# Block-sum attention with a top-1 mixture of experts on one core: route work ahead of the minimum, drains behind gathers, one test that ends the pairs, outputs scaled ahead of the last weight splits

## The chip, the cores and the metric

One Trainium2 chip, one core of it. The metric is the device time of one execution in microseconds; times before and after are medians over several executions. The engines are named as the profile names them: PE (TensorE matmul; PEld is its weight load), DVE (VectorE), ACT (ScalarE), POOL (GpSimd), SP (SyncE). A "q" behind a name is that engine's sequencer: branches, semaphore operations, drains.

## The reference

Attention over 4 batches, 8 heads, 768 positions of width 64: each query sees the keys less than 16 positions away and one summary key (a maximum) and value (a mean) for each block of 32. Its output, 3072 tokens of 512 values, goes through 8 experts, one for each token, and each token's result is scaled by two gates.

```python
k_sum = k.reshape(B, H, nb, block, D).max(axis=3)
v_sum = v.reshape(B, H, nb, block, D).mean(axis=3)
scores_l = scale * q @ k.T          # where |i - j| < 16
scores_s = scale * q @ k_sum.T + log(block)
a = softmax(concat([scores_l, scores_s]))
x = (a @ concat([v, v_sum])).transpose(0, 2, 1, 3).reshape(B * S, H * D)

logits = x @ w_gate
e_idx = argmax(logits, axis=1)
gate_w = softmax(logits)[e_idx]
eom = sigmoid(x @ w_output_gate)
for e in range(E):                   # 8 experts, 512 -> 1024 -> 512
    mask = e_idx == e
    h = maximum(x[mask] @ w1[e], 0)
    out[mask] = gate_w[mask] * eom[mask, e] * (h @ w2[e])
```

## The kernel before

**Attention** (`attention`) works through 24 tiles of 128 queries, six for each batch. The instructions of all engines stand in an order written out by hand: one step of the main loop for each tile, and in a step the scores of the tile two ahead (matmul L329, mask added by DVE into `pr`, L334), the values of tiles that are due (`pv`, L372; `norm`, on DVE), the transposes of this tile's weights (`pt`, L361), the exponent of the next tile on ACT, the minimum of the tile two ahead (`mn`, DVE, L341), and its subtraction from `pr` on POOL (L346). POOL also copies the next queries and keys into order (`nat_q`, `nat_k`, L242). Other work is entered in dictionaries under the step that is to do it: `early` and `put` are run ahead of the minimum, `rts` and `todo` behind it, `end`, `plan` and `pools` at the step's end.

Such other work is:

- `means` and `gather_means`: the block means of the values; matmuls, one of them (`mg`, L269) sorts the rows into place, and ACT copies the result into `mst`. `put_means` copies `mst` into `vw`, which the value matmuls read; one of two copies is DVE's (L215), one ACT's (L217).
- `turn_logits` (`lt` on PE, then `lg`): the gate logits of two tiles.
- `route`, a generator that is run a step at a time, one batch (768 tokens) at once. Step 1 is eight DVE operations on 48 or 6 elements per partition, from `mx` (L431) over `fi` (L435) and `oh` (L439) to `o1` (L445). Step 2 is the exponents on ACT, the counting matmuls `rk` and `tot` on PE (L452, L457), and five DVE operations (`at` to `posi`). Step 3 is seven more (`ssum`, `eo`, `pair`), and behind it come six scatters into the lists of tokens in DRAM.
- `table`: three steps of DVE operations that find which expert and which rows the first three slots take.

**The experts** work on slots of up to 256 tokens of one expert. Slots 0 to 2 take tokens of the first two batches; slot 0 is spread over the end of attention. Item numbers below are slot numbers: 0 to 8 are always full, and then come pairs of one full and one half item (128 tokens), whose number depends on the routing; in this input there are three pairs. A full item runs `first` (eight blocks `hp`, L937 to L939, each with w1 and x split in a high and a low part), then `second` (`yp`, L1080 to L1082), with the weights of the next slot loaded and split on the way (high part by ACT, L906, low part by DVE, L907, or POOL). At the fourth block of `second`, `take_x` transposes the next slot's rows out of `xg` (`xp`, L919), and `fetch` starts gathering the rows of the slot after that into `xg` (an indirect DMA on POOL's queue, L873). `write` scales the two halves of the output (`y`: DVE for the first, ACT for the second, L1100, L1102) and scatters them to `out` (POOL's queue, L1103). `fetch_list` gathers a slot's list of tokens (`lst`, L858), also on POOL's queue. A `drain` on POOL stands behind `fetch_list` at the start of `full` and `half` (L947, L1025): POOL's next instruction waits until what it issued has ended.

From slot 2 on, only POOL's order is as written (`run`); for the other engines, and for all of them within the pairs, a scheduler sets the order. The number of pairs is known at run time only: `rest` loads three counts into registers of every engine, and `pairs`, `left`, `more` and `more_half` nest tests on them. An arm that is taken falls through to the next instruction; a failed test jumps. The profile shows the tests at L1121, the counts' loads at L1115 and the end of the program at L1177.

Of the kernel before, what the change touches and what calls it, by code (L numbers as in the profile page):

```python
# [11 lines left out]
F32 = mybir.dt.float32  # L12
# [185 lines left out]
def attention(tc, const, sa, sb, st, ps, dr, q, k, v, id_sb, c_sb, wg_sb, x_dr, l_dr, rt, moe, table, begin, swap):  # L198
# [333 lines left out]
    early, todo, put, scat, rts, end = {}, {}, {}, {}, {}, {}  # L532
# [10 lines left out]
    for b in range(B):  # L543
        first = live[TB * b]
        for m in range(3):
            later(first - (3 if b == 0 else 4) + m, lambda b=b, m=m: means(b, m), early if b == 0 and m == 2 else todo)
        later(first - 1, lambda b=b: gather_means(b), early)
# [22 lines left out]
    for i, (b, tok) in enumerate(tiles[:n - AHEAD]):  # L570
# [56 lines left out]
    assert not plan and not pools and not scat and not early and not end  # L627
# [14 lines left out]
    for x in rts.pop(t):  # L642
        x()
    assert not todo.pop(t, None) and not put and not todo and not rts
# [119 lines left out]
def rest_slots(tc, const, c_sb, rt):  # L764
# [13 lines left out]
    cnt = const.tile([P, 4], F32, name="cnt")  # L778
    counts = const.tile([P, 4], I32, name="counts")

    def order(inc):
        full, half, pair, past = (cnt[:, i:i + 1] for i in range(4))
# [8 lines left out]
        nc.vector.scalar_tensor_tensor(past, full, half, half, ALU.is_gt, ALU.mult)  # L791
        nc.vector.tensor_copy(counts, cnt)
# [18 lines left out]
class Experts:  # L811
# [133 lines left out]
    def full(self, s, nxt_n=2):  # L945
        self.fetch_list(s + 3, 2)
        self.tc.nc.gpsimd.drain()  # L947
# [73 lines left out]
    def half(self, s, nxt_n=2):  # L1021
# [3 lines left out]
        self.tc.nc.gpsimd.drain()  # L1025
# [28 lines left out]
        with self.tc.manual_schedule(engines={mybir.EngineType.PE}):  # L1054
# [8 lines left out]
            for j in range(NF):  # L1063
# [50 lines left out]
    def rest(self, counts):  # L1114
        n = [self.tc.nc.values_load(counts[0:1, i:i + 1], min_val=0, max_val=m) for i, m in enumerate((MOST - STRAIGHT, E, E))]  # L1115
# [9 lines left out]
    def pairs(self, s, k, n_full, n_half, n_pair):  # L1125

        if k == max(min(h, most(h) - STRAIGHT) for h in range(E + 1)):
            return self.left(s, k, n_full, n_half)
        with self.branch(self.tc.If(n_pair > k)) as c:
            self.full(s, 1)  # L1130
            self.half(s + 1)
            self.pairs(s + 2, k + 1, n_full, n_half, n_pair)
        with self.branch(c.Else()):
            self.left(s, k, n_full, n_half)
# [46 lines left out]
```

## Time and profile before

| | us |
|---|---|
| median of 3 executions | 546.37 |
| their range | 544.06 to 549.19 |
| the profiled execution | 551.64 |
| its span, first to last instruction | 549.9 |

| engine | busy us | share of the span |
|---|---|---|
| PE | 490.5 | 89% |
| DVE | 386.0 | 70% |
| ACT | 321.9 | 59% |
| POOL | 252.0 | 46% |

The page shows the span in 40 equal slices of 13.7 us; a digit is the busy share in tenths, and PEclk is the granted clock of PE in tenths.

```
PE   6788998997967979999799999999999999999940
DVE  2758589889967669997457567665667677785860
POOL 8645555576767757873332240313304225224220
PEclk8899999998979999999799999999999999999985
```

Attention fills slices 1 to 13, the items slices 14 to 38. Digits below 9 on PE stand in attention, in slices 14 to 20 here and there, and in the last two.

### The profile page before, as it was taken

Reading aid. Unit: us, or ns where it says so; the run is one execution under the profiler, and the core shown is the slowest. Engines: PE = TensorE matmul, PEld = TensorE weight load, DVE = VectorE, ACT = ScalarE, POOL = GpSimd, SP = SyncE. Lnnn points to the kernel's source line nnn. Section 1 sums busy time; section 2 is a strip of 40 time slices with the busy share of each in tenths; the row PEclk is TensorE's granted clock in tenths of the full one; section 3 lists DMA queues with packets and bytes.
Section 4 is the critical chain, followed back from the end, with each engine's and each line's share of the span. In section 5 each row is a group of like instructions: output and inputs, shape, how many; then the busy total and the mean of one; then the engine's idle time right before and its main releaser. Section 6 shows DMA issues by size and latency. Waiting matters only on the chain.

```text
span 549.9 us, 12665 instructions
## 1 busy us (share of the span) xinstructions
PE 490.5 (89%) x4396; PEld 411.4 (75%) x4396; DVE 386.0 (70%) x799; ACT 321.9 (59%) x628; POOL 252.0 (46%) x281
## 2 busy tenths in 40 slices
PE   6788998997967979999799999999999999999940
PEld 6556685685546777979698988989899879879730
DVE  2758589889967669997457567665667677785860
ACT  3566686485557665374446556555565585775650
POOL 8645555576767757873332240313304225224220
PEclk8899999898979999999799999999999999999985
DMA  9999948658017379835737658485673966796651
GB/s 235 193 241 213 273 108 224 157 136 162 24 37 230 117 239 349 235 75 175 277 131 254 224 185 303 138 288 186 237 257 112 323 245 210 253 336 207 211 162 18
DMA packets 105684, 109.71 MB, mean 200 GB/s; under 512 B 43150, under 2 KB 67886, under 8 KB 105584
## 3 DMA queue, kind: packets, MB, share of 16 engines
q1 hardware_dynamic: 96208, 88.20, 54.6%
q0 software_dynamic: 9376, 20.35, 11.9%
q8 instruction: 42, 0.69, 0.6%
q14 instruction: 58, 0.48, 0.5%
HBM read 98.33 MB, written 13.59 MB: 204 GB/s over the span
## 4 chain that ended last, share of the span: by engine, by line
PE 65%; DVE 11%; ACT 7%; issue 7%; DMA 4%; POOL 2%; POOLq 0%; SPq 0%; DVEq 0%; ACTq 0%
PE hp L939 8%; PE hp L937 8%; PE hp L938 7%; PE yp L1080 7%; PE yp L1082 7%; PE yp L1081 7%; PE pv L372 3%; PE sp L329 3%; PE pt L361 3%; PE xp L919 2%; PE ms L260 2%; PE xtr L398 1%; DVE mn L341 1%; DVE pr L334 1%; PE qtr L287 1%
## 5 line engine op out<-in xcount | busy, mean ns | idle before, releaser
L906 ACT ACTIVATE w2h<-raw 128x512 fp32r<-128x512 f32 x128 | 77.2, 629 | 63.7 <-PE yp L1082 26.3
L937 PE MATMUL hp<-xhl,w1h 128*128 128x256 f32 x384 | 109.3, 286 | 1.2 <-issue 1.2
L938 PE MATMUL hp<-xhl,w1h 128*128 128x256 f32 x384 | 109.1, 284 | 1.1 <-DVE xhl L922 1.1
L907 DVE TENSOR_TENSOR w2l<-raw,w2h 128x512 fp32r<-128x512 f32 x123 | 83.0, 700 | 37.6 <-ACT w2h L906 31.9
L939 PE MATMUL hp<-xhl,w1l 128*128 128x256 f32 x384 | 109.1, 284 | 0.0
L873 POOL DMA_INDIRECT xg<-x_dr,lst x34 | 37.8, 1113 | 139.9 <-PE xp L919 106.6
L1080 PE MATMUL yp<-w2h,hh 128*128 128x512 f32 x216 | 87.6, 406 | 0.0
L1082 PE MATMUL yp<-w2h,hl 128*128 128x512 f32 x216 | 85.9, 398 | 0.1
L1081 PE MATMUL yp<-w2l,hh 128*128 128x512 f32 x216 | 85.8, 397 | 0.0
L907 DVE TENSOR_TENSOR w1l<-raw,w1h 128x512 fp32r<-128x512 f32 x117 | 76.9, 706 | 11.7 <-ACT w1h L906 9.1
L938 PEld LDWEIGHTS hp<-xhl,w1h 128*128 128x128 f32 x384 | 74.0, 193 | 2.7 <-DVE xhl L922 1.3
L937 PEld LDWEIGHTS hp<-xhl,w1h 128*128 128x128 f32 x384 | 73.8, 193 | 2.7 <-issue 1.7
L906 ACT ACTIVATE w1h<-raw 128x512 fp32r<-128x512 f32 x128 | 71.8, 621 | 5.6 <-DMA raw<-in_moe_w_dram 3.6
L940 ACT ACTIVATE hh<-hp 128x256 fp32r<-128x256 f32 x96 | 36.4, 380 | 65.9 <-PE hp L939 55.6
L939 PEld LDWEIGHTS hp<-xhl,w1l 128*128 128x128 f32 x384 | 74.0, 193 | 0.0
L941 DVE SCALAR_TENSOR_TENSOR hl<-hp,hh 128x256 fp32r<-128x256 f32 x96 | 39.4, 420 | 41.4 <-ACT hh L940 32.0
L346 POOL TENSOR_TENSOR pr<-pr,mn 128x960 f32<-128x960 f32 x24 | 43.0, 1793 | 53.5 <-DVE lg L215 18.7
L1103 POOL DMA_INDIRECT out_dram<-y,lst x27 | 31.6, 1171 | 51.0 <-DVE y L1100 38.8
L217 ACT ACTIVATE pT<-pt 120x512 f32<-120x512 f32 x48 | 26.8, 595 | 39.8 <-PE pt L361 35.2
L1082 PEld LDWEIGHTS yp<-w2h,hl 128*128 128x128 f32 x216 | 41.1, 191 | 9.7 <-issue 0.5
L1080 PEld LDWEIGHTS yp<-w2h,hh 128*128 128x128 f32 x216 | 41.5, 192 | 8.1
L1081 PEld LDWEIGHTS yp<-w2l,hh 128*128 128x128 f32 x216 | 41.4, 192 | 7.9
(198 smaller groups left out, 857.8 us busy)
## 6 DMA issues: line engine op xcount, KB each, us to landing
raw<-in_moe_w_dram SPq DMA_DIRECT2D x256, 256.0 KB
raw_k<-in_k_dram SPq DMA_DIRECT2D x12, 512.0 KB
raw_q<-in_q_dram SPq DMA_DIRECT2D x12, 512.0 KB
x_dr<-xs POOLq DMA_DIRECT2D x24, 256.0 KB
vw<-in_v_dram SPq DMA_DIRECT2D x44, 128.0 KB
vw<-in_v_dram SPq DMA_DIRECT2D x33, 64.0 KB
vw<-in_v_dram POOLq DMA_DIRECT2D x11, 64.0 KB
xg<-x_dr,lst POOLq DMA_INDIRECT x34
```

What stands on the lines that cost most here:

```text
L346: nc.gpsimd.tensor_tensor(pr, pr, mns.pop(i).unsqueeze(2).to_broadcast([P, H, W]), ALU.subtract)
L873: nc.gpsimd.indirect_dma_start(out=self.xg[t], out_offset=None, in_=self.x_dr[0:rows, :], in_offset=bass.IndirectOffsetOnAxis(ap=self.list ...
L906: nc.scalar.activation(hi, raw, AF.Copy)
L907: (lo_by or nc.vector).tensor_tensor(lo, raw, hi.bitcast(F32), ALU.subtract)
L937: nc.tensor.matmul(hp, lhsT=w_h[:, fs], rhs=self.xh[:, c, :], start=c == 0, stop=False)
L938: nc.tensor.matmul(hp, lhsT=w_h[:, fs], rhs=self.xl[:, c, :], start=False, stop=False)
L939: nc.tensor.matmul(hp, lhsT=w_l[:, fs], rhs=self.xh[:, c, :], start=False, stop=c == NC - 1)
L940: nc.scalar.activation(hh[:, j, :], hp, AF.Relu)
L941: nc.vector.scalar_tensor_tensor(hl[:, j, :], hp, 0.0, hh[:, j, :].bitcast(F32), ALU.max, ALU.subtract)
L1080: nc.tensor.matmul(y, lhsT=hh[:, j, tk], rhs=w_h, start=j == 0, stop=False)
L1081: nc.tensor.matmul(y, lhsT=hh[:, j, tk], rhs=w_l, start=False, stop=False)
L1082: nc.tensor.matmul(y, lhsT=hl[:, j, tk], rhs=w_h, start=False, stop=j == NF - 1)
```

## The change

It has seven parts:

1. `gather_means` of batches 1 to 3 is run at the end of the step before the one it was run in.
2. `turn_logits` and step 2 of `route` (the counting matmuls) go into a new dictionary `mid`, run behind `norm` and ahead of the transposes of the weights.
3. Steps 1 and 3 of `route` and the three steps of `table` go into a new dictionary `small`, run behind `put` and ahead of the minimum.
4. At a step's end `pools` is run ahead of `plan`: on POOL a slot's list or rows are fetched ahead of the clearing of `xg` or of a weight's split.
5. The drains at the start of `full` and `half` are gone; `second` has one, behind the gathers of rows that it issues. Half items have none.
6. A fifth count, `more`, is the number of pairs, plus one if there are more full than half items or the other way round. `pairs` is wrapped in a test on it.
7. `write` stands ahead of the last weight fetches in `second` and in `half`.

```diff
-        later(first - 1, lambda b=b: gather_means(b), early)
+        later(first - 1 - (b > 0), lambda b=b: gather_means(b), end if b else early)
...
+    for i in range(3):
+        later(live[2 * TB - 1] + 4 + i, table, small)
     plan = {
-        live[2 * TB - 1] + 4: [table], live[2 * TB - 1] + 5: [table], live[2 * TB - 1] + 6: [table, begin],
+        live[2 * TB - 1] + 6: [begin],
...
             norm(t)
+        for x in mid.pop(i, []):
+            x()
         turn_p(i)
         exps(i + 1)
-        for x in early.pop(i, []) + put.pop(i, []):
+        for x in early.pop(i, []) + put.pop(i, []) + small.pop(i, []):
             x()
         smallest(i + AHEAD)
...
-                    later(i + 2, lambda tb=tb, ttok=ttok: turn_logits(tb, ttok), rts)
+                    later(i + 2, lambda tb=tb, ttok=ttok: turn_logits(tb, ttok), mid)
...
-                    later(i + soon + x, lambda tb=tb: route_to(tb), rts)
+                    later(i + soon + x, lambda tb=tb: route_to(tb), mid if x == 1 else small)
...
-        for x in end.pop(i, []) + plan.pop(i, []) + pools.pop(i, []):
+        for x in end.pop(i, []) + pools.pop(i, []) + plan.pop(i, []):
...
+        nc.vector.scalar_tensor_tensor(more, full, half, pair, ALU.not_equal, ALU.add)
...
     def full(self, s, nxt_n=2):
         self.fetch_list(s + 3, 2)
-        self.tc.nc.gpsimd.drain()
...
     def half(self, s, nxt_n=2):
...
-        self.tc.nc.gpsimd.drain()
...
+                if j == NF - 1:
+                    self.write(s, yp)
                 if j >= 2:
                     self.fetch_w(2, nxt, [j - 2] if j < NF - 1 else [j - 2, j - 1, j])
-            self.write(s, yp)
...
     def second(self, s, n, hh, hl, nxt, nxt2, nxt_n):
...
                 self.fetch(nxt2, 2)
+                self.tc.nc.gpsimd.drain()
             self.second_block(j, yp, hh, hl)
+            if j == NF - 1:
+                self.write(s, yp)
             self.fetch_w(2, nxt, [j])
-        self.write(s, yp)
...
-    def pairs(self, s, k, n_full, n_half, n_pair):
+    def pairs(self, s, k, n_full, n_half, n_pair, n_more):
 
-        if k == max(min(h, most(h) - STRAIGHT) for h in range(E + 1)):
-            return self.left(s, k, n_full, n_half)
-        with self.branch(self.tc.If(n_pair > k)) as c:
...
+        with self.branch(self.tc.If(n_more > k)):
+            if k == max(min(h, most(h) - STRAIGHT) for h in range(E + 1)):
+                return self.left(s, k, n_full, n_half)
+            with self.branch(self.tc.If(n_pair > k)) as c:
```

What this does to the order of instructions, at three places. A row is a line, an operation, and the tiles it writes and reads, with their numbers.

DVE in the step that runs step 1 of batch 0's route. Before:

```order
L215 COPY vw_170<-mst_1025 24x8x64
L341 TENSOR_REDUCE mn_1348<-pr_1304 128x8
L431 TENSOR_REDUCE mx_1354<-lg_919 128x6
L433 TENSOR_TENSOR d_1356<-lg_919,mx_1354 128x48
L435 SCALAR_TENSOR_TENSOR fi_1358<-d_1356,c_sb 128x48
L437 TENSOR_REDUCE first_1360<-fi_1358 128x6
L439 TENSOR_TENSOR oh_1362<-c_sb,first_1360 128x48
L441 CAST ohb_1364<-oh_1362 128x48
L443 TENSOR_TENSOR os_1366<-lg_919,oh_1362 128x48
L445 TENSOR_REDUCE o_1368<-os_1366 128x6
L334 TENSOR_TENSOR pr_1427<-sp_1409,c_sb 128x480
```

And in the changed kernel:

```order
L215 COPY vw_170<-mst_965 24x8x64
L431 TENSOR_REDUCE mx_1348<-lg_903 128x6
L433 TENSOR_TENSOR d_1350<-lg_903,mx_1348 128x48
L435 SCALAR_TENSOR_TENSOR fi_1352<-d_1350,c_sb 128x48
L437 TENSOR_REDUCE first_1354<-fi_1352 128x6
L439 TENSOR_TENSOR oh_1356<-c_sb,first_1354 128x48
L441 CAST ohb_1358<-oh_1356 128x48
L443 TENSOR_TENSOR os_1360<-lg_903,oh_1356 128x48
L445 TENSOR_REDUCE o_1362<-os_1360 128x6
L341 TENSOR_REDUCE mn_1364<-pr_1304 128x8
L334 TENSOR_TENSOR pr_1427<-sp_1409,c_sb 128x480
```

The minimum `mn`, which POOL's subtraction of this step waits for, moved from ahead of the eight route operations to behind them.

POOL at the start of slot 2: lists 3, 5, 4, the writes of slots 1 and 2 (`lst_2802` and `lst_2805` are their lists), and the rows of slots 3 and 4. Drains aren't rows of such a listing; the one of slot 2 stood ahead of the first `out_dram` row. Before:

```order
L858 DMA lst_3662<-l_dr,rowib 128x2 x2
L858 DMA lst_3763<-l_dr,rowib 128x2 x2
L1103 DMA out_dram<-y,lst_2802 3072x512 x2
L873 DMA xg_2472<-x_dr,lst_3662 128x512
L873 DMA xg_2473<-x_dr,lst_3662 128x512
L858 DMA lst_3757<-l_dr,rowib 128x2 x2
L873 DMA xg_2472<-x_dr,lst_3757 128x512
L873 DMA xg_2473<-x_dr,lst_3757 128x512
L1103 DMA out_dram<-y,lst_2805 3072x512 x2
```

And in the changed kernel (here the lists of slots 1 and 2 are `lst_2780` and `lst_2783`):

```order
L863 DMA lst_3663<-l_dr,rowib 128x2
L863 DMA lst_3764<-l_dr,rowib 128x2
L1109 DMA out_dram<-y,lst_2780 3072x512 x2
L878 DMA xg_2475<-x_dr,lst_3663 128x512
L878 DMA xg_2476<-x_dr,lst_3663 128x512
L863 DMA lst_3758<-l_dr,rowib 128x2 x2
L878 DMA xg_2475<-x_dr,lst_3758 128x512
L878 DMA xg_2476<-x_dr,lst_3758 128x512
L1109 DMA out_dram<-y,lst_2783 3072x512 x2
```

The rows stand as before but for the two lists in front, which now alternate, one issue each in turn; what changed is the drain, which stands behind the gathers of slot 4's rows.

POOL between two pairs: the write of a half item's output and what follows it. Before:

```order
L873 DMA xg1_2473<-x_dr_74,lst16_6658 128x512
L1103 DMA out_0_dram<-y_7100,lst14_6209 3072x512
L1121 COMPARE_AND_BRANCH
L858 DMA lst18_7107<-l_dr_75,rowib_3622 128x2 x2
L873 DMA xg1_2473<-x_dr_74,lst17_6930 128x512
```

And in the changed kernel:

```order
L878 DMA xg1_2476<-x_dr_74,lst16_6674 128x512
L1109 DMA out_0_dram<-y_7103,lst14_6225 3072x512
L1127 COMPARE_AND_BRANCH x2
L863 DMA lst18_7123<-l_dr_75,rowib_3623 128x2 x2
L878 DMA xg1_2476<-x_dr_74,lst17_6946 128x512
```

A pair now begins with two tests, the new one on `n_more` and the old one on `n_pair`. After the last pair the old program failed a test on `n_pair`, one on `n_full` and one on `n_half` before it came to the resets of the semaphores; the new one fails the test on `n_more`.

More of the change, by code (lines that the diff above doesn't have):

```diff
@@ L530, in attention @@
     live[n - 1] = n
-    early, todo, put, scat, rts, end = {}, {}, {}, {}, {}, {}
+    early, todo, put, scat, rts, end, small, mid = {}, {}, {}, {}, {}, {}, {}, {}
     def later(i, work, when=todo):
@@ L641, in attention @@
         x()
-    for x in rts.pop(t):
+    for x in mid.pop(t, []) + rts.pop(t, []):
         x()
-    assert not todo.pop(t, None) and not put and not todo and not rts
+    assert not todo.pop(t, None) and not put and not todo and not rts and not mid
     store_x(t - 1)
@@ L777, in rest_slots @@
     nc.vector.tensor_tensor(t[:, E:2 * E], rt["base"], r[:, E:2 * E], ALU.is_gt)
-    cnt = const.tile([P, 4], F32, name="cnt")
-    counts = const.tile([P, 4], I32, name="counts")
+    cnt = const.tile([P, 5], F32, name="cnt")
+    counts = const.tile([P, 5], I32, name="counts")
     def order(inc):
-        full, half, pair, past = (cnt[:, i:i + 1] for i in range(4))
+        full, half, pair, more, past = (cnt[:, i:i + 1] for i in range(5))
         seq = c_sb[:, C_SLOT:C_SLOT + NITEM]
@@ L1114, in rest @@
     def rest(self, counts):
-        n = [self.tc.nc.values_load(counts[0:1, i:i + 1], min_val=0, max_val=m) for i, m in enumerate((MOST - STRAIGHT, E, E))]
+        n = [self.tc.nc.values_load(counts[0:1, i:i + 1], min_val=0, max_val=m) for i, m in enumerate((MOST - STRAIGHT, E, E, E + 1))]
         self.pairs(EARLY + STRAIGHT, 0, *n)
@@ L1123, in branch @@
         self.expert, self.lists = kept
-    def pairs(self, s, k, n_full, n_half, n_pair):
-        if k == max(min(h, most(h) - STRAIGHT) for h in range(E + 1)):
-            return self.left(s, k, n_full, n_half)
-        with self.branch(self.tc.If(n_pair > k)) as c:
[L1130 to L1134, printed above, removed]
+    def pairs(self, s, k, n_full, n_half, n_pair, n_more):
[3 more added lines that the diff above has]
+            with self.branch(self.tc.If(n_pair > k)) as c:
+                self.full(s, 1)
+                self.half(s + 1)
+                self.pairs(s + 2, k + 1, n_full, n_half, n_pair, n_more)
+            with self.branch(c.Else()):
+                self.left(s, k, n_full, n_half)
     def left(self, s, k, n_full, n_half):
```

2 lines of the change are left out of this document (1 added, 1 removed).

## Prediction

> **What bounds the kernel now.** I read the page's head and its chain of work first: the span, and who carries the end.
>
> ```profile
> span 549.9 us, 12665 instructions
> PE 65%; DVE 11%; ACT 7%; issue 7%; DMA 4%; POOL 2%; POOLq 0%; SPq 0%; DVEq 0%; ACTq 0%
> ```
>
> PE carries two thirds of the chain, so a term counts only where PE waits, where its clock falls, or after its last matmul. The view by windows says where that is. Each row gives the window in us, its length, the busy time of PE, PE's weight loads, DVE, ACT and POOL (instructions in brackets), then PE's granted clock, the DMA share and GB/s.
>
> ```profile
> 50.00:100.00 50.00, 48.11 (x766) 35.23 (x763) 38.95 (x93) 32.50 (x62) 26.74 (x29) 0.97 0.89 209
> 100.00:150.00 50.00, 44.59 (x652) 30.97 (x652) 44.92 (x109) 32.80 (x63) 33.58 (x42) 0.97 0.50 113
> 150.00:180.00 30.00, 22.73 (x314) 17.75 (x314) 22.62 (x56) 18.76 (x32) 19.48 (x23) 0.83 0.41 133
> 290.00:420.00 130.00, 130.00 (x830) 117.49 (x829) 85.89 (x151) 76.19 (x152) 36.46 (x34) 1.00 0.64 221
> 420.00:442.00 22.00, 22.00 (x137) 19.70 (x136) 14.07 (x26) 12.19 (x25) 7.38 (x8) 1.00 0.68 240
> 516.00:550.00 34.00, 12.41 (x61) 9.42 (x59) 13.94 (x22) 12.14 (x23) 5.66 (x5) 0.75 0.38 110
> ```
>
> From 290 to 442 PE is full at full clock, and the change alters nothing on PE there: whatever it does to POOL, ACT and DVE in these items is worth nothing unless it makes PE wait. PE has slack to win in attention (1.9, 5.4 and 7.3 us idle in the first three rows), around slot 2, and in the tail.
>
> **Tail: one test ends the pairs.** The rows of the last 20 us, by line: median and ends of the duration in ns, first and last start.
>
> ```profile
> 531.90 1.81 POOL L1103 DMA_INDIRECT out_dram<-y,lst  x1 [3.05 <-DVE y L1100]
> L1121 POOLq COMPARE_BRANCH  x1: 63/63/63, 531.7 to 531.7; - x1
> L1121 POOLq COMPARE_BRANCH  x2: 45/48/50, 536.2 to 540.0; - x2
> L1121 POOLq EVENT_SEMAPHORE  x4: 17/43/43, 542.6 to 542.9; - x4
> L1177 POOLq DRAIN  x3: 46/103/620, 548.4 to 549.6; - x3
> L1121 PEldq COMPARE_BRANCH  x2: 4918/5528/6137, 530.9 to 535.8; - x2
> L1121 PEldq COMPARE_BRANCH  x1: 5053/5053/5053, 542.2 to 542.2; - x1
> L1121 DVEq COMPARE_BRANCH  x7: 43/55/67, 420.1 to 542.2; - x7
> L1115 PEldq TENSOR_LOAD <-counts x3: 302/306/497, 413.7 to 414.7; - x3
> ```
>
> The last write is issued by 533.7, yet the span ends at 549.9: 16 us of hops. On POOL the tests at 531.7, 536.2 and 540.0 are each followed by nothing for 2.6 to 4.5 us, until the resets at 542.6, and a last hop leads to the drain at 548.4. These are taken jumps: three failed tests (no fourth pair, no fourth full, no fourth half) and the jump over the reset. With n_more = 3 the first failed test leads straight to the reset, and two hops fall out. On POOL that is 540.0−536.2 = 3.8 and 542.6−540.0 = 2.6, together 6.4 us; on PE, 4.9 and 6.1, together 11.1. POOL ends the span, and the resets can't pass before the last write has landed, so I take −6, with bounds −4 (the 3.8 hop alone) and −11 (PE's two). The cost: seven to eight more tests per engine that fall through, at 43 to 67 ns (DVE's row) about 0.4 us, one load of a count, 0.3 to 0.5 us, and one DVE operation on one element; they lie in stretches where PE's queue is full (420 to 442), so they cost nothing there.
>
> **Drains behind gathers.** The row of the drains, two rows of waits (us, times, longest), and the stretch of slot 2.
>
> ```profile
> L947 POOLq DRAIN  x10: 3662/5510/12423, 244.2 to 495.3; - x10
> L1025 POOLq DRAIN  x3: 7592/8893/9094, 427.1 to 504.0; - x3
> POOL xg L873 <- PE xp L919: 106.6, 10, 12.6
> PE xp L919 <- DMA xg<-x_dr,lst: 3.0, 2, 2.4
> 250.60 0.74 DVE L1100 TENSOR_SCALAR y<-yp,lst 128x512 f32<-128x512 f32 x1
> 257.49 1.02 POOL L1103 DMA_INDIRECT out_dram<-y,lst  x1 [7.79 <-DVE hl L941]
> 260.12 1.05 POOL L873 DMA_INDIRECT xg<-x_dr,lst  x1 [0.30 <-issue]
> 261.48 6.43 DMA xg<-x_dr,lst
> 257.00:274.00 17.00, 14.01 (x65) 11.64 (x64) 8.59 (x14) 7.58 (x14) 8.39 (x8) 0.80 0.83 292
> ```
>
> The first drain of the program sits at 244.2 and lasts 12.4 us, ahead of slot 1's write, though its y was ready at 251.3 (250.60 + 0.74). Behind it slot 3's rows are fetched at 260.1, land 6.43 us after the second issue, and PE waits for them 3.0 us in two pieces; then its clock falls (0.80 over 257 to 274). I price the clock as window × (1 − clock) × PE's busy share: 17 × 0.20 × 0.82 = 2.8 us. Without the drain the write starts at about 251.6 instead of 257.5, the fetch 5.9 us earlier, and the rows are there some 3 us before PE asks. So up to 3.0 + 2.8 = 5.8 goes. I take −5.5, with bounds 0 (the landing stays late since 292 GB/s run there) and −5.8.
>
> In the later items POOL waits for PE's xp 106.6/10 = 10.7 us each and PE is full: the drains there cost nothing, and neither does their going. Put behind the gathers, a drain holds up the next write of y and the next list; it may last 10.7 us, plus the 5.5 of the old drain that is gone, before POOL's round is longer than an item. The halves lose theirs (8.9 us) altogether.
>
> **Attention: route, table and means ahead of the minimum.** Rows of small DVE operations (min/median/max ns), two rows of one moment, a POOL copy, the waits of this stretch, and two windows.
>
> ```profile
> L435 DVE SCALAR_TENSOR_TENSOR fi<-d,c_sb x4: 207/1678/1895, 89.1 to 212.1; 128x48 f32<-128x48 f32 x4
> L470 DVE TENSOR_SCALAR eo<-eo x4: 159/966/1768, 102.9 to 220.9; 128x6 f32<-128x6 f32 x4
> 88.88 1.82 POOL L346 TENSOR_TENSOR pr<-pr,mn 128x960 f32<-128x960 f32 x1 [1.63 <-DVE mx L431]
> 89.09 1.68 DVE L435 SCALAR_TENSOR_TENSOR fi<-d,c_sb 128x48 f32<-128x48 f32 x1
> L242 POOL COPY nat_q<-raw_q x10: 1036/1048/1057, 26.4 to 154.4; 128x1024 f32<-128x1024 f32 x10
> DVE vw L215 <- ACT mst L217: 11.3, 4, 4.0
> PE pt L361 <- DVE km L301: 3.7, 1, 3.7
> PE pv L372 <- ACT vw L217: 2.2, 1, 2.2
> PE lp L407 <- DVE pr L334: 2.0, 2, 1.9
> PE qtr L287 <- DVE inc4a L694: 0.9, 1, 0.9
> PE rk L452 <- DVE ohb L441: 0.6, 1, 0.6
> PE tot L457 <- DVE pr L334: 0.6, 1, 0.6
> 125.00:134.00 9.00, 5.10 (x48) 3.25 (x48) 8.57 (x23) 4.75 (x11) 5.47 (x9) 0.81 0.88 172
> 157.00:168.00 11.00, 8.00 (x72) 6.37 (x76) 9.32 (x22) 6.81 (x12) 6.04 (x7) 0.53 0.27 89
> ```
>
> The same operation on 48 elements takes 0.21 us alone and 1.68 us beside POOL's subtract: fi runs from 89.09 to 90.77, and the subtract from 88.88 to 90.70. The subtract starts when DVE's minimum is done, and today the route's steps stand just behind it. Put ahead of the minimum they meet a POOL that hasn't its operand yet. So the DVE stretches behind the minimum shrink, and what waits on them comes sooner: the PE waits above that name km, pr, ohb and inc4a (3.7 + 2.0 + 0.6 + 0.6 + 0.9 = 7.8). The means gathered a step earlier take away the ACT wait of DVE's vw (11.3 us) and PE's 2.2. Together 10.0 us; the clock beside them, priced as above, 9 × 0.19 × 0.57 = 1.0 and 11 × 0.47 × 0.73 = 3.8. The ceiling is 14.8.
>
> Not all of it goes. The route's own work stays on DVE, the minimum, and with it subtract and exponent, comes some 2 us later in the four steps concerned, and the next wait is then for pr itself. And turn_logits moved behind norm puts lt on PE earlier, where its copy on ACT may be late. The mean's matmul, a step earlier, stands nearer to the copy that feeds it. For these I leave 0.4 of the ceiling and take −9, with bounds −14 and, as nothing excludes a late exponent that PE waits for, +2. The list, xg and w1l moves on POOL late in attention change places of work that is 1 to 1.5 us each: w1l(raw_0_5) is later by two list issues of 1.3 to 1.5 each and its raw buffer held as long. ACT's y, one place earlier in the straight items, lies where PE is full: 0.
>
> The Trainium skill, "SBUF — State Buffer", section "Who interferes with whom", states that a DVE operation with two inputs in SBUF contends with any GpSimd operation that reads SBUF, and that the first holds the shared ports for its whole length; the two rows at 88.88 and 89.09 agree (1.68 against 0.21). By it the copies of 1.05 us hold DVE as well as the subtract does, so that an operation moved ahead of the minimum can be lengthened by up to 1.05 in place of 1.79. As an estimate by that page the attention term would be 0.41 of mine, −3.7.
>
> **The sum.** −6 −5.5 −9 = −20.5. The profiled execution took 551.64 us, 1.7 outside its span; it stands 5.3 above the median of the runs, 546.37 (544.06 to 549.19), one per cent, and shows no wait of its own that the others could lack, so I carry the difference over: span 529.4, execution 531.1, median 525.9.
>
> **Rivals.**
> - **B, the copies take the subtract's place.** nat_q's copies (1.05 us) and DVE's own later minimum eat the attention gain down to −2. For it: 44.9 of 50 us of DVE are busy from 100 to 150, so a moved wait has little room. Against it: the copy stands behind the previous subtract, most of a step before the moved operations. −6 −5.5 −2 gives 532.9.
> - **C, another wait holds slot 3's rows.** The rows of xg can't be fetched until slot 1's y is written and the DMA queues, 0.83 busy there, serve them; PE then waits at xp as now. −6 −9 gives 531.4. Against it: out_dram was released by nothing but the drain (y 251.3, write 257.5).
> - **D, slower: the drain behind the gathers is the new bound.** It waits for the rows and delays each next write and list. It decides once a drain is longer than 10.7 + 5.5 = 16.2 us. Then each of some eight items pays what slot 3 pays now, 3.0 + 2.8: +46 − 20.5 gives 572. Against it: the longest now is 12.4, and that one stands behind the last scattered writes of the lists.
> - **E, the tail keeps its length.** The jump goes as far as three hops went, or the wait for the last write decides (issued until 533.7, landing in some 3 to 6 us, as xg's 6.43). The tail gives −1: 530.9.
>
> **How the numbers follow.** A change of under 1 per cent, 5.5 us, can hardly be told from none in this kernel. Chances: the forecast 0.58, B 0.22, C 0.09, E 0.07, D 0.04. The predicted time is the forecast's, 526. Its own range is 516 to 533: −11 −5.8 −14 gives 515.6, and −4 −5.5 −4 gives 532.9. The range of 514 to 539 reaches past B, C and E to two of them at once (B and E: −1 −5.5 −2 gives 537.9); it leaves out D and the mixtures of three. Faster 0.86: all of the forecast, and B, C and E but for 0.10 of their upper ends (B with C gives −6 −2, 538.4; with E too −1 −2, 543.4; at the attention term's bound of +2 four more). Same 0.10, slower 0.04.
>
> **What would show it.** Right: the time from the last write's issue to the end falls from 16.2 to about 10, with one POOL test after 531 and no hop between it and the resets; no drain ahead of slot 1's write, PE's wait for xg at slot 3 gone, and the clock of that stretch near 1; fi, eo and their like near 0.2 us in three of four places; the waits for km, pr and vw halved, and PE's clock over 157 to 168 above 0.8. Wrong: PE below 130.00 of 130 in the straight items (D), POOL copies beside lengthened route operations (B), xg's landing still ending PE's wait at slot 3 (C), POOL's resets still waiting for the last write (E).

## The result, and the profile after

| | before | after |
|---|---|---|
| median of 20 executions, us | 547.15 | 540.69 |
| range, us | 544.06 to 554.53 | 537.38 to 548.99 |
| profiled execution, us (span) | 551.64 (549.9) | 538.93 (537.1) |

The ratio is 0.9891, with a 95% interval from 0.9862 to 0.9919: faster by 1.1 per cent, some 6 us, where 20.5 were forecast. The spans of the two profiles differ by 12.8 us, since the profiled execution of before was a long one of its kind (551.64 against a median of 547.15) and that of after a short one (538.93 against 540.69); so single profiles can't carry the sum here, and the experiments below give each part its own ratio.

The head of the page after, and its chain of work:

```profile
span 537.1 us, 12679 instructions
PE 61%; DVE 11%; ACT 9%; DMA 7%; issue 5%; POOL 4%; DVEq 0%; POOLq 0%; ACTq 0%
```

PE's share of the chain fell from 65 to 61%, and DMA's rose from 4 to 7%: something besides PE now carries part of the time. The view by windows after (columns as in the prediction) says where not:

```profile
50.00:100.00 50.00, 48.27 (x776) 34.91 (x772) 38.76 (x106) 35.18 (x68) 25.96 (x28) 1.00 0.83 198
100.00:150.00 50.00, 45.79 (x664) 31.16 (x663) 35.97 (x105) 30.65 (x60) 32.39 (x41) 0.97 0.55 123
150.00:180.00 30.00, 20.41 (x274) 16.55 (x273) 22.78 (x48) 17.77 (x30) 21.57 (x24) 0.82 0.43 133
247.00:290.00 43.00, 43.00 (x284) 39.27 (x283) 28.68 (x53) 24.29 (x50) 17.25 (x15) 1.00 0.72 246
290.00:420.00 130.00, 130.00 (x855) 118.75 (x855) 84.52 (x152) 73.91 (x149) 37.67 (x36) 1.00 0.63 214
```

The row of slots 2 and 3 before:

```profile
247.00:290.00 43.00, 39.27 (x251) 35.85 (x252) 25.30 (x46) 19.52 (x40) 14.95 (x14) 0.92 0.58 199
```

Slots 2 and 3 (247 to 290) are now full at full clock (43.00 for 39.27 us busy, 1.00 for 0.92), as the straight items stay. DVE's busy time from 100 to 150 fell by 9 us, and PE gained 1.2 there. But from 150 to 180 PE is less busy than before (20.4 against 22.7), and its clock is no better (0.82 against 0.83). To see where time is won and lost, the starts of the same PE work in the two traces stand side by side (us):

```
PE work                                before    after   after - before
first values matmul                     38.67    37.95    -0.72
transposes pt of tile 19               160.07   154.27    -5.80
first transposes of gathered rows      179.06   178.72    -0.34
first expert matmul                    182.40   184.02    +1.62
slot 2, among its first matmuls        254.05   252.34    -1.71
after the transposes of slot 3's rows  276.91   269.14    -7.77
last half item, its transposes         523.33   516.80    -6.53
end of the span                        549.9    537.1    -12.8
```

Attention wins 5 us by tile 19 and has lost them at the first expert matmul. The last 2 us of that go between the first transposes of rows (−0.34) and the first expert matmul (+1.62), and there PE's clock is low: from 178 to 184 us it is 0.58 after and 1.00 before, and the transposes take 1.91 us for 1.04. Slot 3 wins 6.1, the tail 6.3; 1.2 are lost in the pairs between them. The tail and the drains after, first POOL's last row in the view by time:

```profile
524.74 1.21 POOL L1109 DMA_INDIRECT out_dram<-y,lst  x1 [2.30 <-DVE y L1106]
```

then the resets and the drains in the view by line (ns: least, median, longest; first and last start):

```profile
L1127 POOLq EVENT_SEMAPHORE  x4: 17/43/3772, 527.4 to 531.4; - x4
L1094 POOLq DRAIN  x10: 3701/5846/9703, 264.3 to 489.0; - x10
```

and POOL's wait for PE in the view of waits (us, times, longest):

```profile
POOL xg L878 <- PE xp L924: 105.2, 13, 12.4
```

The resets, which before started at 542.6 without waiting, now start at 527.4, and one of them lasts 3.77 us; the last of them starts at 531.4, 5.4 us after the last write's issue ended at 525.95. In the program's order that is a wait for the last write, though the trace doesn't show its landing. From the end of that issue to the end of the span it is now 11.2 us, and was 16.2. The first drain is at 264.3, none lasts over 9.7 us, and POOL still waits 105 us for PE: no item got longer. Last, the small operations of the route in the view by line:

```profile
L435 DVE SCALAR_TENSOR_TENSOR fi<-d,c_sb x4: 207/208/1881, 88.0 to 210.7; 128x48 f32<-128x48 f32 x4
L470 DVE TENSOR_SCALAR eo<-eo x4: 157/164/165, 98.6 to 219.5; 128x6 f32<-128x6 f32 x4
```

The medians fell from 1678 and 966 ns to 208 and 164: they did get out of the way of POOL's subtraction, as foreseen. It was worth next to nothing.

### The profile page after: what moved, and what is told of

It is laid out like the page before. It is cut to its first block, busy times and chain, and to the rows that moved or that the text cites. A ratio compares the mean times of both kernels' runs of the same rounds, so it can differ in the third digit from the quotient of the medians.

```text
span 537.1 us, 12679 instructions
## 1 busy us (share of the span) xinstructions
PE 487.1 (91%) x4396; PEld 408.7 (76%) x4396; DVE 375.7 (70%) x800; ACT 322.1 (60%) x628; POOL 255.0 (47%) x281
## 4 chain that ended last, share of the span: by engine, by line
PE 61%; DVE 11%; ACT 9%; DMA 7%; issue 5%; POOL 4%; DVEq 0%; POOLq 0%; ACTq 0%
PE yp L1084 8%; PE yp L1086 8%; PE yp L1085 8%; PE hp L942 8%; PE hp L943 8%; PE hp L944 8%; PE xp L924 3%; PE pt L361 2%; DMA raw<-in_moe_w_dram 2%; PE pv L372 2%; PE sp L329 2%; DMA l_dr<-pair,posi 2%; ACT pr L350 2%; ACT pT L217 2%; DMA l_dr<-fill 2%
## 5 line engine op out<-in xcount | busy, mean ns | idle before, releaser
L878 POOL DMA_INDIRECT xg<-x_dr,lst x34 | 39.8, 1172 | 111.3 <-PE xp L924 105.2
L912 DVE TENSOR_TENSOR w1l<-raw,w1h 128x512 fp32r<-128x512 f32 x117 | 80.4, 736 | 13.7 <-ACT w1h L911 12.2
```

Of the source, the lines that this page charges most:

```text
L878: nc.gpsimd.indirect_dma_start(out=self.xg[t], out_offset=None, in_=self.x_dr[0:rows, :], in_offset=bass.IndirectOffsetOnAxis(ap=self.list ...
L912: (lo_by or nc.vector).tensor_tensor(lo, raw, hi.bitcast(F32), ALU.subtract)
```

## The experiments

All ratios are to the kernel before, run on the same chip. The runs were made in batches on several chips, and the median of the kernel before lay between 547.4 and 553.3 us in them; where two versions ran in one batch, their own medians are the better comparison.

### One part alone

The one test, alone (the diff of `pairs`, and the fifth count):

```diff
+        with self.branch(self.tc.If(n_more > k)):
```

> The kernel before with the fifth count and the one test that ends the pairs, and nothing else. The two profiles show 6.3 us less from the last matmul to the end. Theory 1 (the tail is a fixed price, paid in every run): -6.3 us, ratio 0.988 to 0.989, so that it alone is the whole of the change's 6.5 us. Rival (the tail of the profiled run before was a long one, and jumps vary from run to run): -3 us, ratio 0.994 to 0.995.

0.9863 (0.9821 to 0.9905), some 7.5 us: theory 1, and if anything more than the whole change gives (the intervals overlap).

The drains, alone:

```diff
-        self.tc.nc.gpsimd.drain()
+                self.fetch(nxt2, 2)
+                self.tc.nc.gpsimd.drain()
```

> The kernel before with the drains moved behind the gathers of rows, and nothing else. Theory 1 (the stall at slot 3 is in every run of the kernel before): -6 us, ratio 0.989, and no wait of PE for the gathered rows at slot 3. Rival (that stall is rare, and the profiled run had it by chance, which is why it stands 4.5 us above the median of 20): -1 us, ratio 0.997 to 1.000, while the trace still shows the write of slot 1 earlier.

0.9896 (0.9851 to 0.9941), some 5.7 us: theory 1. Each of the four profiles with the old drains (the kernel before, the one test alone, and attention's parts in two runs) has PE waiting 3.0 to 4.2 us for slot 3's rows. This is the view of PE's waits from 245 to 275 us with the one test alone, the old drains in place:

```profile
PE xp L920 <- DMA xg<-x_dr,lst: 3.6, 1, 3.6
PE hp L939 <- DVE xhl L923: 1.4, 1, 1.4
```

In the run with the drains moved alone, the same view has no row at all.

Attention's parts, without and with POOL's new order:

```diff
+        later(first - 1 - (b > 0), lambda b=b: gather_means(b), end if b else early)
+        for x in early.pop(i, []) + put.pop(i, []) + small.pop(i, []):
...
+        for x in end.pop(i, []) + pools.pop(i, []) + plan.pop(i, []):
```

> The kernel before with the means, the route and the table moved in attention, POOL's lists and rows left behind the weight splits. Theory 1 (POOL's new order gives the gain back: the 4.43 us split on DVE beside POOL's split and subtraction): attention keeps most of the 6.7 us that it leads by at 168 us, -4 to -5 us, ratio 0.991 to 0.993, and no split on DVE over 2.5 us. Rival (slot 0's rows set the end of attention: scatters of the lists, list 0, gather, transposes, whatever PE does before them): -1 us, ratio 0.997 to 1.000, with the first transposes of gathered rows at 178 to 179 us.

> As the run before it, and POOL's lists and rows also ahead of the weight splits, as in the change. Theory 1: 3 to 4 us slower than without that order, -1 us against the kernel before, and the 4.43 us split on DVE is there. Rival (slot 0's rows set the end): within 1 us of the run without that order, or faster by up to 1.5 us, since the gather is issued earlier.

1.0024 (0.9983 to 1.0065) and 1.0054 (1.0019 to 1.0089). Neither forecast of a gain came true: the moved attention alone gains nothing, and with POOL's new order it is slower by 3 us. The first had no split on DVE over 2.5 us, as theory 1 wanted, and no gain either; its rival, that the end is fixed, was nearer. The second has the split of 4.43 us again, but stands only 0.3 per cent above the first, with overlapping intervals.

### Parts together

The one test and the drains, as in the two diffs above:

> The kernel before with the one test and the drains behind the gathers, attention and the writes as before. Theory 1 (the two are independent): the product of the two ratios measured alone, 0.9863 x 0.9896 = 0.976, about -13 us and some 6 us below the whole change: the change's attention parts then cost that much. Rival (the two share a gain, or the attention parts are worth something beside them): ratio 0.985 to 0.990, no faster than the whole change.

0.975 (0.9713 to 0.9788), where the product of the two ratios is 0.976: the two are independent, and together 1.4 per cent below the whole change (0.9891). By the ratios the rest of the change costs that much beside them. But the whole change was timed in another batch, and the two medians themselves are hardly apart (539.84 and 540.69); a comparison within one batch stands below, under the scatters.

With the outputs scaled ahead:

```diff
+            if j == NF - 1:
+                self.write(s, yp)
             self.fetch_w(2, nxt, [j])
-        self.write(s, yp)
```

> The one test, the drains, and the outputs scaled ahead of the last splits. Theory 1 (in full items PE is full, and nothing waits for y): within 0.3 per cent of the run without the write moved, ratio 0.975 to 0.979. Rival (the write moved ahead costs the part of the loss that the attention parts, +0.5 per cent alone, don't explain): ratio 0.981 to 0.985, with the loss in the pairs or in slots 1 to 3.

0.9746 (0.97 to 0.9791): the outputs ahead of the last splits cost nothing.

With the means, or with the route and the table (the first and the second line of the diff of attention's parts):

> The one test, the drains, and the means gathered a step earlier, route and table as before. Theory 1 (the means are the good half: DVE's and PE's waits for the copy go, nothing is put ahead of a minimum): -1 to -2 us against the run without it, ratio 0.972 to 0.975. Rival (slot 0's rows set the end of attention whatever PE saves): ratio 0.976 to 0.979.

> The one test, the drains, and route and table ahead of the minimum, means and POOL's order as before. Theory 1 (the later minimum makes subtraction and with it POOL's scatters of batch 1's lists later by 1.5 to 2 us, and list 0 waits for their landing): +2 to +3 us against the run without it, ratio 0.980 to 0.983, list 0 issued 1.5 us or more later against the scores of the same step. Rival (the route ahead of the minimum saves what its lengthened operations cost): ratio 0.966 to 0.972.

0.9803 (0.9762 to 0.9843) with the means, 0.9764 (0.9734 to 0.9794) with the route and the table. The first lies above both of its forecasts, so the means are not the good half; the second lies between its two. Neither is below 0.975, but both intervals overlap with its own, so which of the two costs more is open.

### What gives attention's lead back

The chain of work after, from 150 to 185 us (start, us, what), without its small pieces:

```profile
153.26 1.16 DVE mn L341
...
154.52 7.61 DMA l_dr<-pair,posi
...
162.96 2.41 DMA lst<-l_dr,rowia
165.37 1.00 POOL xg L839 x2
166.37 1.93 POOL pr L346
168.33 1.00 ACT pr L350
...
171.33 4.32 issue
175.65 1.21 DVE pr L334 x2
...
178.93 1.71 PE xp L924 x8
```

Before, the same stretch ran through PE itself and DVE:

```profile
163.89 1.08 PE lp L407 x8
164.97 1.90 PE qtr L287 x8
166.87 0.85 PE xtr L398 x4
167.73 0.98 PE sp L329 x32
168.71 1.08 PE pv L372 x32
```

with the last scatter and list 0 in POOL's rows, list 0 without a wait for a landing:

```profile
153.44 0.96 POOL L480 DMA_INDIRECT l_dr<-pair,posi  x1 [0.19 <-issue]
163.17 1.02 POOL L858 DMA_INDIRECT lst<-l_dr,rowia  x1 [0.30 <-DVE early L759]
```

Now it runs through POOL's queue: the last scatter of batch 1's lists takes 7.6 us to land, list 0 waits for it, and behind list 0 stands a subtraction (166.31) whose minimum had been done since 159.7. Then comes a piece of 4.32 us that is DVE's split of a weight:

```profile
171.29 4.43 DVE L912 TENSOR_TENSOR w1l<-raw,w1h 128x512 fp32r<-128x512 f32 x1 [3.47 <-ACT w1h L911]
```

and POOL beside it:

```profile
162.96 1.16 POOL L863 DMA_INDIRECT lst<-l_dr,rowia  x1 [4.14 <-DMA l_dr<-pair,posi]
171.52 1.28 POOL L912 TENSOR_TENSOR w1l<-raw,w1h 128x512 fp32r<-128x512 f32 x1
172.74 1.79 POOL L346 TENSOR_TENSOR pr<-pr,mn 128x960 f32<-128x960 f32 x1
174.47 0.60 POOL L391 DMA_DIRECT2D x_dr<-xs  x1
175.10 1.75 POOL L912 TENSOR_TENSOR w1l<-raw,w1h 128x512 fp32r<-128x512 f32 x1
```

and in the view of PE's waits from 140 to 200 us, of which the largest rows after are

```profile
PE lp L407 <- DVE pr L334: 5.0, 1, 5.0
PE sp L329 <- ACT qt L217: 2.8, 1, 2.8
PE pv L372 <- ACT vw L217: 0.6, 1, 0.6
```

and before

```profile
PE lp L407 <- DVE pr L334: 3.1, 2, 1.9
PE pv L372 <- ACT vw L217: 2.2, 1, 2.2
```

DVE's split, 0.69 us elsewhere, gets through only when POOL's split and subtraction, one against the other, are over, and by the times also the issue behind them (174.47 to 175.07; the split ends 0.65 later). PE waits 5.0 us for the sum that DVE does next. All rows of PE in this view add up to 9.8 us before and 9.9 after. Four runs tried to undo the one or the other.

```diff
-        for x in end.pop(i, []) + pools.pop(i, []) + plan.pop(i, []):
+        for x in end.pop(i, []) + (plan.pop(i, []) + pools.pop(i, []) if i == n - AHEAD - 3 else
+                                   pools.pop(i, []) + plan.pop(i, [])):
```

> The whole change, but at the one step where slot 0's rows are gathered POOL's weight split stands ahead of the gather again, as before the change. Theory 1 (the gather pushes POOL's split against the next subtraction, and DVE's own split is blocked for both, 4.43 us, while PE waits 5.04 us for the sum behind it): -3 us against the whole change, ratio to the kernel before 0.982 to 0.985, no split on DVE over 2.5 us near 171 us. Rival (slot 0's rows set the end): no gain, 0.988 to 0.991, the first transposes of gathered rows at 178 to 179 us as now.

0.9831 (0.9772 to 0.989): the time that theory 1 gave, but its sign in the trace is not there. DVE's split still lasted 4.01 us, at 167.4 now, with 3.0 us of PE's waiting behind it in place of 5.0. So the order may matter, by about 0.6 per cent with overlapping intervals, but not by ridding DVE of the block. Nor does the block alone decide the time: the run above with the route and the table had a split of 3.94 us at 166.2, in POOL's old order, and came to 0.9764, and the run of attention's parts alone had none and gained nothing.

The old order at every step:

```diff
-        for x in end.pop(i, []) + pools.pop(i, []) + plan.pop(i, []):
+        for x in end.pop(i, []) + plan.pop(i, []) + pools.pop(i, []):
```

> The whole change without POOL's new order (lists and rows behind the clearing and the splits, as before the change). Theory 1 (the new order is what blocks DVE's split): 2 to 3 us below the whole change, ratio 0.983 to 0.986, with no split on DVE over 2.5 us near 171 us. Rival: same as the whole change, 0.988 to 0.991.

0.9868 (0.9816 to 0.992), with one split of 2.78 us: between the two, and not to be told from either.

```diff
-    pools = {live[2 * TB - 1] + 6: [lambda: moe.fetch_list(0, 2)], n - AHEAD - 3: [lambda: moe.fetch(0, 2)],
+    pools = {live[2 * TB - 1] + 7: [lambda: moe.fetch_list(0, 2)], n - AHEAD - 2: [lambda: moe.fetch(0, 2)],
```

> The whole change, but list 0 and the gather of its rows stand one step later on POOL, each behind a subtraction that it held up before (list 0 waits 4.1 us for the lists' scatters to land, with a subtraction behind it whose minimum was done 6.5 us before it started). Theory 1 (POOL's wait for the scatters, not the rows' arrival, gives the lead back): that subtraction starts at about 160 instead of 166 us, the lead of 5 us at 157 us lasts to the first expert matmul, -4 to -6 us against the whole change, ratio 0.978 to 0.981. Rival (the rows' arrival sets the end, or the split on DVE): 0.986 to 0.991.

0.9898 (0.9859 to 0.9937). The subtraction started at 163.5 instead of 166.3 and no split lasted over 1.25 us, so both waits were gone. The rows then came late, and PE waited for them:

```profile
PE xp L924 <- DMA xg<-x_dr,lst: 4.2, 2, 3.4
```

Theory 1 falls: the one wait is exchanged for the other.

And the same without the means:

```diff
-        later(first - 1 - (b > 0), lambda b=b: gather_means(b), end if b else early)
+        later(first - 1, lambda b=b: gather_means(b), early)
```

> As the second run of this set, with the means gathered where they were before the change. Theory 1 (the means gathered earlier cost something, as the 0.5 per cent of one run would have it): 1 to 3 us below that run. Rival (that half per cent was chance, since the same attention code spread over 8 us between five profiles): within 1.5 us of it, or above it, since DVE's wait for the copy is back.

0.9899 (0.9844 to 0.9954), the same as with the means moved: the rival. The cost of the means that the batch above hinted at was not confirmed.

### The place of the scatters

For each profile the start of some work was taken from the start of its first values matmul. `posi`, the last of the route's operations that the scatters of batch 1 need on DVE's side of step 2, moved; what POOL does with it did not:

```
                                  posi done  last scatter  list 0   gather  first xp  first hp
old attention (mean of five)         98.1       115.9       124.8    132.7    140.3     143.6
the change                           93.3       116.6       125.0    131.2    140.8     146.1
attention's parts with POOL's order  92.4       115.7       124.2    130.3    139.9     144.9
attention's parts alone              95.0       118.3       127.5    133.8    138.0     144.3
```

The route's result is there 3 to 6 us earlier, and the scatters, the list and the first expert matmul are not, the first transposes in the last row alone (by 2.3 us): POOL's scatters are entered under their steps, and what stands ahead of them on POOL is the same. Four runs moved the scatters themselves.

```diff
-                    later(i + soon + 2 + x // (1 if tb == 0 else 3), lambda tb=tb: scatter(tb), scat)
+                    later(i + soon + 2 + x // (1 if tb == 0 else 6), lambda tb=tb: scatter(tb), scat)
```

> The whole change with the old order at the gather of slot 0's rows, and all six scatters of batch 1's lists on POOL in the step of the first three, ahead of the next subtraction. Theory 1 (the chain last scatter, landing, list 0, its landing, gather, first transposes sets the end of attention): the last scatter 2 to 2.5 us earlier against the first values matmul, the list, the gather and the first transposes with it, ratio 0.978 to 0.981 (0.9831 without). Rival (PE and the subtractions set it, which stand 3.8 us later at that place): ratio 0.983 to 0.990.

0.982 (0.978 to 0.9859). The last scatter came 2.6 us earlier than without (114.2 against 116.7 in the measure of the table), but list 0 did not (123.2 against 122.6): subtractions and a copy stand between them on POOL. The ratio lies between the two forecasts and the sign of theory 1 is missing: no gain to speak of.

```diff
+                    later(i + soon + 2 + (x if tb == 0 else 1 + x // 3), lambda tb=tb: scatter(tb), scat)
```

> The same with batch 1's scatters one step later on POOL, three and three. Theory 1 (the scatters' chain sets the end): list 0 and the first transposes 5 to 7 us later, ratio 0.993 to 0.998. Rival (there is slack between the lists and the first transposes): 0.983 to 0.987.

0.9877 (0.9823 to 0.9931), slower by 0.5 per cent where 1 to 1.5 were expected. In the profile the scatters came 7.4 us later, list 0 8.1 later (130.7), and the first expert matmul 7.3 later (149.8 against 142.5). POOL's row of list 0:

```profile
169.23 0.98 POOL L863 DMA_INDIRECT lst<-l_dr,rowia  x1 [5.55 <-DMA l_dr<-pair,posi]
```

So later scatters do move the end, in the profile by as much as they move. The ratio's loss is smaller, with an interval that overlaps that of the run without, which is of another batch. In its own batch stands the run with the six together, which differs from it by the place of the scatters alone: there the last scatter comes 10.0 us earlier, the first expert matmul 6.9 (142.9 against 149.8), and the median is 538.5 against 543.9 us, though two executions of the later one lie within the range of the other. That is the clearest sign here that this chain has hardly any slack against the end of attention.

The six together in the old attention, with the one test and the drains:

> The one test and the drains with attention as before the change, and the six scatters together. Theory 1 (the same chain sets the end there): first transposes 2 us earlier than 140.3 us after the first values matmul, the mean of five profiles of that attention code; ratio 0.971 to 0.973 (0.975 without). Rival (in the old attention PE's own lateness sets the end, since list 0 waits for nothing but POOL): 0.975 to 0.979.

0.9727 (0.9688 to 0.9766), median 533.38, the fastest version of all and faster than both kernels. Its first transposes of rows are 4.1 us ahead of the mean of the old attention (136.1 against 140.3 in the table's measure), twice what was expected, its first expert matmul 2.5 (141.1). Against 0.975 without, the intervals overlap. Within the batch its executions (531.97 to 534.31) lie wholly below those of the whole change with the six together (537.99 to 539.77, median 538.47): beside the one test, the drains and the same six scatters, the rest of the change (POOL's old order kept at the gather of slot 0's rows) costs 5 us.

And that with the route and the table ahead of the minimum and POOL's new order everywhere but at the gather of slot 0's rows:

> The one test, the drains, route and table ahead of the minimum, the means as before, the old order at the gather of slot 0's rows and the six scatters together: what the runs so far favour. Theory 1: ratio 0.970 to 0.974. Rival (no order of attention's small work is worth more than the one test and the drains alone): 0.975 to 0.980.

0.9781 (0.9733 to 0.9829), median 536.24: the rival. It is not faster than the run before it; no version with a moved part of attention's work beats the ones with the old attention.

## Why the prediction was wrong

**The tail** was right in kind and in size: −6 was taken, −7.5 measured alone, and within the bounds. The hops fell out, and the wait in the resets (3.77 us), which rival E named, is what ends now; it limits the gain but doesn't take it. That the size fits is luck in part: in the profiles POOL's stretch from the test ahead of the last write to the resets fell by 8.0 us (531.7 to 542.6 before, 524.5 to 527.4 after) where 6.4 were worked out, and the one from the resets to the end grew by 2.4 (7.3 to 9.7). The "seven to eight more tests" of the prediction are the number of all tests of an engine: there were 7 and are 8, which changes nothing in the sum.

**The drains** were right: −5.5 taken, −5.7 measured. PE's wait at slot 3 and the low clock behind it went together, so C is out. The drain behind the gathers lasts up to 9.7 us and holds up nothing that PE waits for (130.00 of 130 us busy in the straight items); D is out.

**Attention** is the step that failed: "I leave 0.4 of the ceiling and take −9". Without POOL's order the parts measure +0.2 per cent (−0.2 to +0.7), with it +0.5 (+0.2 to +0.9), so +3 us for −9. The ceiling added up waits of PE, and the clock beside them, as if each moved the end of attention. The small operations did become short, and some waits went: that of DVE's vw fell from 11.3 to 4.0 us, that of PE's values for it from 2.2 to 0.6, that of pt for km from 3.7 to 0.8. Others came in their place: rk waits 2.2 for km (0.6 for ohb before), the scores 2.8 for qt, lp 5.0 for pr (3.1). The clock's 4.8 us didn't come either: it is 0.81 from 125 to 134 as before, and though it rose from 0.53 to 0.75 from 157 to 168, over 150 to 180 it is 0.82 for 0.83. PE was 5.1 us ahead at tile 19 in the profile, counted from its first values matmul. But a wait of PE counts only until another chain has to be met, and one was near: scatters, list 0, gather, transposes of slot 0's rows, on POOL and its DMAs. No row of it was read for the prediction. From the last scatter to the first transposes it takes 24.2 us after and 25.6 before (178.72 − 154.52 and 179.06 − 153.44), so there was hardly room for PE to come earlier, and the chain of work went over to it as soon as PE did. That later scatters move the end was seen in the profiles (7.4 us for 7.3) and in the times of the two runs that differ by their place alone; that an earlier chain lets the moved work gain was not, since list 0 didn't come earlier with the scatters. Why the parts lose, and don't only win nothing, stays open: the split of 4.43 us, the wait of 5.0 behind it and the clock of 0.58 lie there, but without that split the parts stand at +0.2 per cent in place of +0.5, with overlapping intervals.

The second thing missed is in the sentence that set the moves of lists and splits on POOL at "1 to 1.5 us each". What was counted is the issue; what counts is the wait in it. A list's gather waits for scatters to land (7.6 us), and everything behind it on POOL waits too: subtraction, exponent, transposes. In the profile after, POOL itself waits 4.1 us there. For the drains the prediction asked what stands behind the waiting instruction; for list 0 it didn't.

**Rival B** had the right place, attention, and half the right kind: POOL's work holds a DVE operation with two inputs in SBUF, but the operation is a weight's split of 512 columns, not the route, and POOL's split and subtraction hold it one after the other (4.43 us). The Trainium skill, "SBUF — State Buffer", section "Who interferes with whom", says that the first holds the shared ports for its whole instruction. The trace shows more: DVE's row started at 171.29, ahead of POOL's at 171.52, and still ended last, at 175.72, behind two of POOL's operations that took 1.28 and 1.79. B was priced at 532.9 with −2 left in attention; the loss of 3 us was outside it too.

**The range** took attention at −4 at its own upper end, 532.9, though the prediction's bound for it was +2; the space up to 539 was there for rivals, not for a loss. Of the 1.7 us by which 540.69 lies above 539, 0.8 come from the base: the kernel before has a median of 547.15 in 20 executions, 546.37 in the 3 that the sum started from.

**What stays open.** One by one the three parts give −7.5 − 5.7 + 3.0 = −10.2 us; the whole gives −6 (4.4 to 7.5). Each of the three has an interval of some 2 us to either side, so this may be chance or a loss in company; the batch with the six scatters says that the rest costs 5 us beside the two good parts. Which of means, route and POOL's order costs how much was not settled either: the same old attention took between 209.5 and 217.7 us to the middle of slot 2 in five profiles, as much as what was looked for.

## What to carry to other kernels

Before waits are added up into a gain, find the next chain that has to meet the same point, and read its slack from its own rows: here the scatters, the list and the gather for the first slot. An operation that is moved earlier on one engine wins nothing while its consumer on another engine keeps its place in a hand-written order; move both or none. And on a queue that runs in order, a gather that must wait for a scatter to land costs what stands behind it, not its issue.

Where a program ends in nested tests, count the jumps that are taken after the last useful work: two fewer were worth 1.4 per cent here, as much as any other part of this change, for one DVE operation, one more count to load and one more test.

## What the runs showed of the hardware

An indirect scatter of 128 rows of 8 bytes, the last of six, took 7.6 us by the chain of work from the start of its issue to its landing (154.52 to 162.13), and the gather that waits for it started at 162.96, while issues of such a kind on POOL take 1.0 us each. A weight's split on DVE took 4.43 us beside POOL's work instead of 0.69, and the block went on over two of POOL's instructions and more that stood one against the other; it took 4.43 us again in the run of attention's parts with POOL's order. PE's clock was 0.58 over the 6 us behind a stretch with a wait of 5.0 us. And with the same code the way through attention varied by 8 us between five profiles, from two chips or more, while the straight items repeated to 0.02 us: a change in the first must be timed many times, one in the second shows in a single profile.
